# Reordered lead-in of a routed-attention and MLP-mixer kernel: q's first rows turned ahead of the centroids, one PSUM buffer each for the clusters of k and q

## The chip, the core and the metric

One core of a Trainium2 chip runs the whole kernel. The metric is device time in microseconds (us) of one execution; the kernel before takes 845.08 us, the median of four executions (844.96 to 846.0).

## What is computed

The reference is routed attention followed by an MLP mixer, all in float32. There are 4 batches, 8 heads, 768 positions, 64 elements per head and 16 centroids per head:

```
q_assign = argmax_c (q/|q|) . (centroid_c/|centroid_c|)      # the same for k
scores   = 0.125 * q k^T where q_assign == k_assign, else -1e9
attn     = softmax(scores) @ v                               # heads side by side: x, 768 x 512
u        = x + (relu(x^T @ w_tok1) @ w_tok2)^T
out      = u + relu(u @ w_ch1) @ w_ch2
```

The setup draws all inputs at random; no centroid is zero.

## The kernel before

The work has two parts. The first treats 16 pairs of heads (4 batches by 4 pairs), one after another; the second is the mixer. TensorE works through both almost without a pause. All instructions stand in each engine's queue in the order in which the program issues them, so an instruction that waits holds up everything behind it on its engine.

For a pair of heads the kernel needs q and k turned, with the head's elements on the partitions (the tile `qkT`), and the cluster of each position of q and k as a one-hot row, turned as well (`ohT`). The scores of the pair (line 422) are two products that add up in PSUM: the one-hot rows of k by those of q, where q's are multiplied by a large negative number, and then k by q. k's one-hot rows are inverted, so the first product is zero for positions of the same cluster. ScalarE takes the exponential of each such tile (line 429), VectorE adds them up (line 437), and TensorE multiplies them by v (line 447). One pass of scores has two halves of q (`qh`) by six blocks of k (`j`).

From the second pair on, turning is done by VectorE (line 292, on rows loaded in quarters by line 141) and by DMA (line 347), during the pair before. The first pair has no pair before it, and the function `begin` prepares it in another way, which I call the lead-in:

- The centroids (`cen`, line 795) and the rows of q and k of the first pair (`load_first`, line 365) are loaded. k's four loads stand in SyncE's queue behind the centroids, q's four in ScalarE's queue. Each has one head's share of one half `n` of the rows. Behind k's loads SyncE issues the loads of the second pair (line 141) and of v (line 150).
- Meanwhile TensorE multiplies a tile of zeros by itself (`keep_warm`, line 813), 12 times at first and a few times between later steps.
- `centroids_norm` (lines 244 to 278) works out on VectorE, in 12 short instructions one behind the other, each centroid divided by its norm (lines 247 to 273; the third of these, line 250, keeps the squared norm above 2 to the power of -100). TensorE turns the result (line 277, tile `pc`). `centroids_out` (line 283) copies it in two parts to the tile `cnd`, from which the products with q and k are made, and line 821 copies it whole to `cnT`, which only a fallback reads.
- `turn_first(0)` (line 376) turns the first half of the rows on TensorE, three blocks of k and three of q. VectorE copies k (line 824) and ScalarE q (line 823) out of PSUM to `qkT`.
- `route_products` (line 302) multiplies the centroids by k and q of this half, and `route` (lines 318, 320, 323) finds each row's largest product and writes the one-hot rows, first k's and then q's.
- `turn_first(1)` turns the second half of the rows, and ScalarE copies both (line 830).
- `route_turn_first(0)` (line 386) turns the one-hot rows on TensorE, three blocks of k and three of q in one PSUM tile `po`. Then `route_first_out` has VectorE copy k's (line 396) and q's (line 394, with the multiplication).
- `route_products` and `route` follow for the second half of the rows, and the scores begin. Between the second and the third block of scores, `second_first` turns the one-hot rows of the second half.

Two PSUM pools matter. `ps_av` has two buffers, which its tiles take in turn: the target of `keep_warm`, `pc`, the two `po`, and then products of the next pair and `av`. `ps_sc` has three, for the turned rows, the products `pr` and the scores.

Of the kernel before, what the change touches and what calls it, by code (L numbers as in the profile page):

```python
# [8 lines left out]
F32 = mybir.dt.float32  # L9
BF16 = mybir.dt.bfloat16  # L10
U32 = mybir.dt.uint32
U16 = mybir.dt.uint16
I32 = mybir.dt.int32
# [6 lines left out]
P = 128  # L20
# [7 lines left out]
HJ = NJ // 2  # L28
HS = HJ * P
# [11 lines left out]
BIG = float(2**33)  # L41
# [7 lines left out]
def kernel(  # L49
# [29 lines left out]
    nc = tc.nc  # L79
# [5 lines left out]
    def pool(name, bufs, stack=None, **kw):  # L85
        return (stack or fast).enter_context(
            tc.tile_pool(name=name, bufs=bufs, reuse_waits="tile", **kw)
        )

    ps_av = pool("ps_av", 2, space=PSUM)  # L90
    ps_sc_stack = fast.enter_context(ExitStack())
    ps_sc = pool("ps_sc", 3, ps_sc_stack, space=PSUM)
# [16 lines left out]
    rsmall = pool("rsmall", 1, routing, side="right")  # L109
# [3 lines left out]
    ident = const.tile([P, P], F32, name="ident")  # L113
    identb = const.tile([P, P], BF16, name="identb")
# [3 lines left out]
    ohs = [rsmall.tile([P, 2, NJ, P], BF16, name=f"oh{i}", bufs=1) for i in range(2)]  # L118
# [9 lines left out]
    state = {}  # L128
# [17 lines left out]
    def load_v(g):  # L146
        b, f = divmod(g, NF)
        st = state[g]
        st["va"] = loads.tile([P, 2, NJ, D], F32, name="va")
        nc.sync.dma_start(  # L150
            st["va"], v[b, 2 * f : 2 * f + 2].rearrange("h (p j) d -> p h j d", p=P)
        )
# [91 lines left out]
    def centroids_norm(cen):  # L244
        sq = rsmall.tile([P, D], F32, name="censq")
        ss = rsmall.tile([P, 1], F32, name="ss")
        nc.vector.tensor_tensor(out=sq, in0=cen, in1=cen, op=ALU.mult)
        nc.vector.reduce_sum(out=ss, in_=sq, axis=AX.X)
        lo = rsmall.tile([P, 1], F32, name="lo")
        nc.vector.tensor_scalar_max(out=lo, in0=ss, scalar1=float(2.0**-100))  # L250


        nrm = rsmall.tile([P, 1], F32, name="nrm0")
        nc.vector.tensor_scalar(
            out=nrm.bitcast(I32), in0=lo.bitcast(I32), scalar1=0.5, scalar2=float(0x1FBB6875),
            op0=ALU.mult, op1=ALU.add,
        )
        for it in range(2):
            rr = rsmall.tile([P, 1], F32, name="rr")
            nc.vector.reciprocal(out=rr, in_=nrm)  # L260
            tw = rsmall.tile([P, 1], F32, name="tw")
            nc.vector.scalar_tensor_tensor(
                out=tw, in0=ss, scalar=rr, in1=nrm, op0=ALU.mult, op1=ALU.add
            )
            nrm = rsmall.tile([P, 1], F32, name="nrm")
            nc.vector.tensor_scalar(
                out=nrm, in0=tw, scalar1=(0.5, 0.49984956)[1 - it], scalar2=(0.0, 1e-6)[it],
                op0=ALU.mult, op1=ALU.add,
            )
        rden = rsmall.tile([P, 1], F32, name="rden")  # L270
        nc.vector.reciprocal(out=rden, in_=nrm)
        cn = rsmall.tile([P, 2, D], F32, name="cn")
        nc.vector.tensor_scalar_mul(
            out=cn, in0=cen.unsqueeze(1).to_broadcast([P, 2, D]), scalar1=rden
        )
        pc = ps_av.tile([P, H * C], F32, tag="av", name="pc")
        nc.tensor.transpose(out=pc, in_=cn.rearrange("p i d -> p (i d)"), identity=ident)
        return pc

    def centroids_out(pc):  # L280
        for i in range(2):
            rows = slice(i * D, (i + 1) * D)
            nc.vector.tensor_copy(
                out=cnd[rows, :, i], in_=pc.rearrange("p (f i c) -> p f i c", f=NF, i=2)[rows, :, i]
            )
# [44 lines left out]
    def route_count(g, js=slice(0, NJ), column=None):  # L330


        column = g if column is None else column
        nc.scalar.activation(
            out=rsmall.tile([P, NJ, 2, C], BF16, name="others")[:, js], in_=onehots(g, 1, js),
            func=ACT.Copy, accum_out=cells[:, column : column + 1],
        )
# [16 lines left out]
    def load_first():  # L354
        st = state[0] = {}
        st["T"] = qktp.tile([P, 2, NJ, P], F32, name="qkT")
        st["ohT"] = qktp.tile([P, 2, NJ, P], BF16, name="ohT")
        st["rows"] = [
            work.tile([P, 2, HS], F32, name="ex").rearrange("p a (j h d) -> p a j h d", h=2, d=D)
            for _ in range(2)  # L360
        ]
        for n in range(2):
            for a, src, queue in ((1, k, nc.sync), (0, q, nc.scalar)):
                for h in range(2):
                    queue.dma_start(
                        st["rows"][n][:, a, :, h],
                        src[0, h].rearrange("(p j) d -> p j d", p=P)[:, HJ * n : HJ * n + HJ],
                    )

    def turn_first(n, tiles):  # L370

        st = state[0]
        js = slice(HJ * n, HJ * n + HJ)
        for a in (1, 0):
            for j in range(HJ):
                nc.tensor.transpose(
                    out=tiles[a][:, j * P : (j + 1) * P],
                    in_=st["rows"][n][:, a, j].rearrange("p h d -> p (h d)"), identity=ident,
                )
        return [(st["T"][:, a, js].rearrange("p j t -> p (j t)"), tiles[a]) for a in range(2)]  # L380

    def route_turn_first(n):
        po = ps_av.tile([P, 2, HJ, P], BF16, tag="av", name="po")
        for a in (1, 0):
            for j in range(HJ):
                nc.tensor.transpose(
                    out=po[:, a, j], in_=ohs[0][:, a, HJ * n + j], identity=identb
                )
        return po

    def route_first_out(n, po, a):
        out = state[0]["ohT"][:, a, HJ * n : HJ * n + HJ]
        if a == 0:
            nc.vector.tensor_scalar_mul(out=out, in0=po[:, 0], scalar1=-BIG)  # L394
        else:
            nc.vector.tensor_copy(out=out, in_=po[:, 1])

    def second_first():

        po = route_turn_first(1)  # L400
        for a in (1, 0):
            route_first_out(1, po, a)
        for n in range(2):
            route_count(0, slice(HJ * n, HJ * n + HJ), NPAIR * n)
        nc.vector.tensor_tensor(
            out=cells[:, 0:1], in0=cells[:, 0:1], in1=cells[:, NPAIR : NPAIR + 1], op=ALU.add
        )
        state[0].pop("rows")
# [384 lines left out]
    def begin():  # L793
        cen = rsmall.tile([P, D], F32, name="cen")
        nc.sync.dma_start(cen, centroids.rearrange("h c d -> (h c) d"))
        load_first()

        nc.vector.memset(ones, 1.0)
        warm = rsmall.tile([P, WMAX], BF16, name="warm")
        nc.vector.memset(warm, 0.0)  # L800
        nc.vector.memset(cnd, 0.0)
        nc.scalar.activation(out=rsmall.tile([P, QP], F32, name="expd"), in_=ones, func=ACT.Exp)
        make_identity(nc, ident)
        nc.gpsimd.tensor_copy(out=identb, in_=ident)
        for oh in ohs:
            nc.gpsimd.memset(oh, 0.0)
        load(1)
        load_v(0)
        pw = ps_av.tile([P, HS], F32, tag="av", name="av")

        def keep_warm(n):
            for _ in range(n):
                nc.tensor.matmul(pw, lhsT=warm[:, 0:P], rhs=warm[:, P : P + HS], start=True, stop=True)

        js = [slice(0, HJ), slice(HJ, NJ)]
        keep_warm(12)
        pc = centroids_norm(cen)
        keep_warm(2)
        scs = [ps_sc.tile([P, 2, 512], F32, tag="sc", name="pt") for _ in range(2)]
        centroids_out(pc)  # L820
        nc.scalar.copy(out=cnT, in_=pc)
        tq, tk = turn_first(0, [x[:, 0, 0:HS] for x in scs])
        nc.scalar.copy(out=tq[0], in_=tq[1])
        nc.vector.tensor_copy(out=tk[0], in_=tk[1])
        keep_warm(2)
        pr = ps_sc.tile([P, 2, 512], F32, tag="sc", name="pr")
        route_products(0, pr[:, 0, 0 : HS // 2], js[0])
        pt = ps_sc.tile([P, 2, 512], F32, tag="sc", name="pt")
        for out, src in turn_first(1, [pt[:, a, 0:HS] for a in range(2)]):
            nc.scalar.copy(out=out, in_=src)  # L830
        route(0, js[0])
        keep_warm(3)
        po = route_turn_first(0)
        for a in (1, 0):
            route_first_out(0, po, a)
        route_products(0, pr[:, 1, 0 : HS // 2], js[1])
        route(0, js[1])

# [325 lines left out]
```

## Time and profile before

| | before |
|---|---|
| median of four executions | 845.08 us (844.96 to 846.0) |
| the profiled execution | 845.76 us |
| its span, first to last instruction | 844.0 us |
| mean granted clock of TensorE | 1.000 |
| TensorE busy | 834.3 us (99%) |
| VectorE busy | 501.8 us (59%) |
| ScalarE busy | 374.8 us (44%) |
| first matmul of scores of the first pair | starts at 11.14 us |

The profile is that of one execution. All places in time are microseconds from the first instruction. PE is TensorE's matmuls and PEld its weight loads, DVE is VectorE, ACT ScalarE, POOL GpSimd, and SP SyncE; a "q" behind an engine's name is its sequencer, which issues DMAs. `qkT<-pt` reads: writes tile qkT from tile pt. L422 is line 422. A row of the timeline gives the start, the time to the end of its last instruction, the engine, the line, the operation, the tiles, the shapes, the number of instructions and, in brackets, how long the engine was idle before it and for whom. A row of the chain of waits gives start, length and what the end of the program was waiting for at that time.

### The profile page before, as it was taken

What the parts mean: (1) busy time and instruction counts of PE and PEld (TensorE: products, weight loads), DVE (VectorE), ACT (ScalarE), POOL (GpSimd) and SP (SyncE); (2) the same over time, 40 slices, a digit from 0 to 9 for tenths busy, and PEclk for the clock granted to TensorE, in tenths of its full rate; (3) what the DMA queues carried; (4) which work ended last, traced back from release to release, by engine and by line L of the source; (5) the groups of instructions that cost most, each with busy time, mean ns of one, the idle gap of its engine ahead of it and who ended that gap; (6) DMA issues with size and microseconds to landing.
All of it is one profiled execution on the core that took longest, in us unless ns stands there. A gap on an engine that the chain in (4) does not pass through costs nothing.

```text
span 844.0 us, 10784 instructions
## 1 busy us (share of the span) xinstructions
PE 834.3 (99%) x4102; PEld 507.1 (60%) x4102; DVE 501.8 (59%) x848; ACT 374.8 (44%) x570; POOL 45.6 (5%) x40
## 2 busy tenths in 40 slices
PE   9999999999999999999999999999999999999997
PEld 4444444444444444444577686785876867768676
DVE  6879898989898862893653434423454333443342
ACT  5678777777777762453210352104612035220210
POOL 1001010101101000430000000000000000000000
PEclk9999999999999999999999999999999999999999
DMA  8786666868675412541000040000310012200001
GB/s 152 148 149 143 125 138 123 169 130 159 146 138 125 57 44 69 162 110 29 0 1 1 19 105 27 0 1 19 82 51 0 1 19 47 85 1 0 1 15 64
DMA packets 183963, 60.19 MB, mean 71 GB/s; under 512 B 172768, under 2 KB 176864, under 8 KB 183904
## 3 DMA queue, kind: packets, MB, share of 16 engines
q1 hardware_dynamic: 182304, 59.04, 33.0%
q8 instruction: 34, 0.56, 0.3%
q10 hardware_dynamic: 1600, 0.39, 0.2%
q14 instruction: 25, 0.20, 0.1%
HBM read 34.64 MB, written 6.29 MB: 48 GB/s over the span
## 4 chain that ended last, share of the span: by engine, by line
PE 92%; DVE 5%; DMA 1%; ACT 0%; issue 0%; SPq 0%; DVEq 0%
PE sc L422 18%; PE pX L740 15%; PE pX L689 15%; PE av L447 13%; PE pZ L689 7%; PE pZ L740 7%; PE ph L527 4%; PE pY L740 4%; PE pY L689 4%; PE pu L536 3%; PE small L483 1%; DVE wh L215 1%; PE small L302 1%; DVE wT L220 1%; DVE wh L210 1%; DVE x L539 1%
## 5 line engine op out<-in xcount | busy, mean ns | idle before, releaser
L429 ACT ACTIVATE ex<-sc 128x768 f32<-128x768 f32 x192 | 149.2, 811 | 27.7 <-PE sc L422 16.1
L422 PE MATMUL sc<-qkT 64*128 64x384 f32 x768 | 155.1, 482 | 0.0
L437 DVE TENSOR_TENSOR sum<-sum,ex 128x768 f32<-128x768 f32 x128 | 127.7, 998 | 27.4 <-ACT ex L429 15.2
L447 PE MATMUL av<-ex,va 128*64 128x384 f32 x768 | 127.4, 488 | 0.0
L447 PEld LDWEIGHTS av<-ex,va 128*64 128x64 f32 x768 | 53.8, 137 | 71.7 <-issue 69.0
L422 PEld LDWEIGHTS sc<-qkT 64*128 64x128 f32 x768 | 68.5, 187 | 36.3 <-issue 35.6
L697 ACT COPY p<-pX 128x384 f32<-128x384 f32 x24 | 11.4, 475 | 138.7 <-PE pX L689 120.5
L689 PE MATMUL pX<-uT,wc 128*128 128x384 f32 x192 | 67.4, 487 | 0.0
L422 PE MATMUL sc<-ohT 64*128 64x384 bf16 x384 | 63.3, 324 | 0.5 <-DVE ohT L394 0.2
L689 PEld LDWEIGHTS pX<-uT,wc 128*128 128x128 f32 x192 | 36.2, 190 | 24.7 <-issue 1.0
L454 ACT COPY avrows<-av 128x768 uint16<-128x768 uint16 x32 | 25.5, 796 | 47.1 <-PE av L447 47.1
L227 POOL TENSOR_TENSOR wc<-wT,wup 128x512 int32<-128x512 int32 x24 | 33.0, 1376 | 191.4 <-DVE wT L220 189.7
L527 PE MATMUL ph<-x,wt 128*128 128x512 f32 x96 | 41.9, 594 | 0.8 <-DVE x L539 0.8
L610 ACT COPY uT<-ucols 128x768 uint16<-128x768 uint16 x32 | 33.5, 1051 | 20.7 <-DMA ucols<-urows 20.7
L422 PEld LDWEIGHTS <-ohT 64*128 64x128 bf16 x384 | 20.1, 94 | 35.9 <-issue 11.1
L536 PE MATMUL pu<-h,wt 128*128 128x512 f32 x96 | 41.7, 592 | 0.0
L553 DVE TENSOR_TENSOR c<-pZ,u 128x384 f32<-128x384 f32 x24 | 13.4, 558 | 46.8 <-PE pZ L689 46.8
L708 ACT ACTIVATE hA<-hA 128x384 f32<-128x384 f32 x24 | 12.6, 523 | 63.4 <-DVE hA L553 63.4
L553 DVE TENSOR_TENSOR x<-pX,x 128x256 f32<-128x256 f32 x24 | 10.2, 423 | 42.8 <-PE pX L740 42.8
L689 PE MATMUL pZ<-uTs,w1s 128*128 128x384 f32 x96 | 35.0, 487 | 0.4 <-DVE uTs L550 0.4
L740 PE MATMUL pX<-wc,hA 128*128 128x256 f32 x144 | 35.0, 379 | 0.0
L740 PE MATMUL pZ<-w2s,hS 128*128 128x256 f32 x144 | 35.0, 379 | 0.0
(121 smaller groups left out, 1224.9 us busy)
## 6 DMA issues: line engine op xcount, KB each, us to landing
raw<-in_moe_w_ch_dram SPq DMA_DIRECT2D x24, 512.0 KB, 4.2
va<-in_v_dram SPq DMA_DIRECT2D x16, 384.0 KB, 3.6
out_dram<-x SPq DMA_DIRECT2D x24, 256.0 KB, 2.1
qk<-in_k_dram SPq DMA_DIRECT2D x60, 96.0 KB, 3.8
qk<-in_q_dram SPq DMA_DIRECT2D x60, 96.0 KB, 3.5
raw<-in_moe_w_tok_dram SPq DMA_DIRECT2D x3, 512.0 KB, 4.6
raw<-in_moe_w_tok_dram SPq DMA_DIRECT2D x4, 384.0 KB, 3.8
ucols<-urows SPq DMA_TRANSPOSE x32, 2.8
```

The source lines that it names most:

```text
L227: nc.gpsimd.tensor_tensor(out=dst.bitcast(I32), in0=T, in1=up, op=ALU.add)
L422: nc.tensor.matmul(sc[:, h, 0:HS], lhsT=src[rows, 1, j], rhs=src[rows, 0, js], start=start, stop=not start,)
L429: nc.scalar.activation(out=ex, in_=sc[:, :, 0:HS], func=ACT.Exp, scale=SM_SCALE)
L437: nc.vector.tensor_tensor(out=acc, in0=acc if j > 1 else st["ex", qh, 0], in1=st["ex", qh, j], op=ALU.add)
L447: nc.tensor.matmul(av[h * D : (h + 1) * D], lhsT=st["va"][:, h, j], rhs=ex[:, h], start=(j == 0), stop=(j == NJ - 1),)
L454: nc.scalar.copy(out=st["rows"][:, qh], in_=av.bitcast(U16).rearrange("p (t w) -> p w t", w=2))
L527: nc.tensor.matmul(pf, lhsT=W["tok1"][:, j, t * P : (t + 1) * P], rhs=xs[b][:, j], start=(j == 0), stop=(j == NJ - 1),)
L536: nc.tensor.matmul(pu, lhsT=W["tok2"][:, t, j], rhs=h1s[b][:, t], start=(t == 0), stop=(t == NT - 1))
L553: nc.vector.tensor_tensor(out=dst, in0=a, in1=b, op=ALU.add)
L610: nc.scalar.copy(out=out, in_=pools.pop(("ucols", i)).rearrange("p w j t -> p w (j t)"))
L689: nc.tensor.matmul(psum, lhsT=A[a][:, k, c * P : (c + 1) * P], rhs=R[r][:, k], start=start and k == 0, stop=k == 1, skip_group_check=not s ...
L740: nc.tensor.matmul(psum, lhsT=h2[a][:, k, i * P : (i + 1) * P], rhs=Bw[w][:, 3 * part + k], start=start and k == 0, stop=k == 2, skip_grou ...
```

## The change

Four things are done in the lead-in, and nothing outside of it:

1. One of the first 12 idle multiplications is taken out, and the two between the centroids and the turning. q's first rows are turned ahead of the centroids' products and copied by ScalarE at once; k's are turned behind the centroids. The copy to `cnT` moves behind k's turning.
2. The instruction that keeps the squared norm above a small number is taken out.
3. The second half of the rows is turned with q first and k second. As before, ScalarE's copies stand behind all six.
4. The one-hot rows of k and of q get a PSUM buffer each. The copy of each is issued right behind its three turns; for the first half, ScalarE copies k's (VectorE did it before).

```diff
-        lo = rsmall.tile([P, 1], F32, name="lo")
-        nc.vector.tensor_scalar_max(out=lo, in0=ss, scalar1=float(2.0**-100))
...
-            out=nrm.bitcast(I32), in0=lo.bitcast(I32), scalar1=0.5, scalar2=float(0x1FBB6875),
+            out=nrm.bitcast(I32), in0=ss.bitcast(I32), scalar1=0.5, scalar2=float(0x1FBB6875),
...
-    def turn_first(n, tiles):
+    def turn_first(n, a, out):
 
         st = state[0]
+        for j in range(HJ):
+            nc.tensor.transpose(
+                out=out[:, j * P : (j + 1) * P],
+                in_=st["rows"][n][:, a, j].rearrange("p h d -> p (h d)"), identity=ident,
+            )
         js = slice(HJ * n, HJ * n + HJ)
+        return st["T"][:, a, js].rearrange("p j t -> p (j t)"), out
+
+    def route_turn_first(n):
+
         for a in (1, 0):
+            po = ps_av.tile([P, HJ, P], BF16, tag="av", name="po")
             for j in range(HJ):
...
+                nc.tensor.transpose(out=po[:, j], in_=ohs[0][:, a, HJ * n + j], identity=identb)
+            out = state[0]["ohT"][:, a, HJ * n : HJ * n + HJ]
+            if a == 0:
+                nc.vector.tensor_scalar_mul(out=out, in0=po, scalar1=-BIG)
+            elif n == 0:
+                nc.scalar.copy(out=out, in_=po)
+            else:
+                nc.vector.tensor_copy(out=out, in_=po)
...
-        keep_warm(12)
+        keep_warm(11)
+        scs = [ps_sc.tile([P, 2, 512], F32, tag="sc", name="pt") for _ in range(2)]
+        tq = turn_first(0, 0, scs[0][:, 0, 0:HS])
+        nc.scalar.copy(out=tq[0], in_=tq[1])
         pc = centroids_norm(cen)
-        keep_warm(2)
-        scs = [ps_sc.tile([P, 2, 512], F32, tag="sc", name="pt") for _ in range(2)]
         centroids_out(pc)
+        tk = turn_first(0, 1, scs[1][:, 0, 0:HS])
+        nc.vector.tensor_copy(out=tk[0], in_=tk[1])
         nc.scalar.copy(out=cnT, in_=pc)
-        tq, tk = turn_first(0, [x[:, 0, 0:HS] for x in scs])
-        nc.scalar.copy(out=tq[0], in_=tq[1])
-        nc.vector.tensor_copy(out=tk[0], in_=tk[1])
         keep_warm(2)
         pr = ps_sc.tile([P, 2, 512], F32, tag="sc", name="pr")
         route_products(0, pr[:, 0, 0 : HS // 2], js[0])
         pt = ps_sc.tile([P, 2, 512], F32, tag="sc", name="pt")
-        for out, src in turn_first(1, [pt[:, a, 0:HS] for a in range(2)]):
+        for out, src in [turn_first(1, a, pt[:, a, 0:HS]) for a in (0, 1)]:
             nc.scalar.copy(out=out, in_=src)
         route(0, js[0])
         keep_warm(3)
-        po = route_turn_first(0)
-        for a in (1, 0):
-            route_first_out(0, po, a)
+        route_turn_first(0)
```

More of the change, by code (lines that the diff above doesn't have):

```diff
@@ L368, in load_first @@
                     )
-    def turn_first(n, tiles):
+    def turn_first(n, a, out):
         st = state[0]
+        for j in range(HJ):
[3 more added lines that the diff above has]
+            )
         js = slice(HJ * n, HJ * n + HJ)
+        return st["T"][:, a, js].rearrange("p j t -> p (j t)"), out
+    def route_turn_first(n):
         for a in (1, 0):
+            po = ps_av.tile([P, HJ, P], BF16, tag="av", name="po")
             for j in range(HJ):
[L376 to L383, printed above, removed]
-        for a in (1, 0):
[L385 to L396, printed above, removed]
+                nc.tensor.transpose(out=po[:, j], in_=ohs[0][:, a, HJ * n + j], identity=identb)
[6 more added lines that the diff above has]
+                nc.vector.tensor_copy(out=out, in_=po)
     def second_first():
-        po = route_turn_first(1)
-        for a in (1, 0):
-            route_first_out(1, po, a)
+        route_turn_first(1)
         for n in range(2):
@@ L832, in begin @@
         keep_warm(3)
-        po = route_turn_first(0)
-        for a in (1, 0):
-            route_first_out(0, po, a)
+        route_turn_first(0)
         route_products(0, pr[:, 1, 0 : HS // 2], js[1])
```

## The prediction, written before the changed kernel ran

> **What bounds the kernel now.** I read the page first: busy time by engine, and the shares of the chain of waits.
>
> ```profile
> PE 834.3 (99%) x4102; PEld 507.1 (60%) x4102; DVE 501.8 (59%) x848; ACT 374.8 (44%) x570; POOL 45.6 (5%) x40
> ...
> PE 92%; DVE 5%; DMA 1%; ACT 0%; issue 0%; SPq 0%; DVEq 0%
> ```
>
> TensorE is the bound. A change to the lead-in can only pay by letting the first pair's scores (L422) start earlier; from there TensorE runs to the end. So I looked for what could hold time in place behind the lead-in. TensorE's own waits, in a list for the whole span, are few: 0.8 us at L527, 0.5 at L302, 0.4 at L689, 0.2 at L422, and those of the lead-in. The 0.5 us at L302 (31.48 us) waits for VectorE, whose work goes back through additions and routing to a product that TensorE makes at 21.48 us. It moves along when TensorE does. The others wait for VectorE too, in chains that start with TensorE's results.
>
> Then I read the chain of waits from the start to 13 us:
>
> ```profile
> 2.72 0.24 DVE censq L247
> ...
> 3.24 0.17 DVE lo L250
> ...
> 5.09 0.30 DVE cn L273
> 5.39 0.14 issue
> 5.53 0.45 PE pc L277
> 5.97 0.64 PE av L813 x2
> 6.61 0.95 PE pt L376 x6
> 7.56 0.02 issue
> 7.58 0.49 ACT qkT L823
> 8.07 0.04 issue
> 8.11 0.53 PE pr L302 x8
> ...
> 10.46 0.04 DVE ohT L396
> 10.49 0.24 issue
> 10.73 0.36 DVE ohT L394
> 11.09 0.04 issue
> 11.14 1.79 PE sc L422 x12
> ```
>
> The reader is to see one chain through four engines. The centroids land at 2.70, VectorE normalises them until 5.38, TensorE turns them, does two multiplications of zeros (L813), turns six blocks, ScalarE copies q, and at 8.11 the products begin. Their routing ends in two VectorE copies, one behind the other (L396, L394), and at 11.14 the scores begin. The timeline of the two copies of turned rows shows who is late:
>
> ```profile
> 7.26 0.56 DVE L824 COPY qkT<-pt 128x384 f32<-128x384 f32 x1 [0.79 <-PE pt L376]
> 7.58 0.48 ACT L823 COPY qkT<-pt 128x384 f32<-128x384 f32 x1 [0.75 <-PE pt L376]
> ```
>
> k is copied by 7.82 and q by 8.06: q comes last, though its rows have long been there (ScalarE issues its first two loads at 0.74 and 1.24, with 2.3 and 2.9 us to landing: 3.0 and 4.1).
>
> **The change, step by step** (times in the profiled execution).
>
> *One multiplication less, q turned first.* The twelfth opening multiplication starts at 4.73; in its place the first block of q is turned. Its rows are there since 4.1, 0.6 us of cover. The first two turns of L376 started 0.21 us apart and took 0.42 each (6.41, 6.61). Three end at 4.73 + 0.42 + 0.42 = 5.57. ScalarE's last work before that ends at 4.38, so it copies from 5.61 to 6.09. q then is far from the end of the chain.
>
> *The clamp.* L250 starts at 3.24, the next instruction at 3.43: 0.19 us go, all on the path. `cn` ends at 5.19 instead of 5.38. TensorE started `pc` 0.15 us after that, so at 5.34; three turns before it occupy TensorE until 4.73 + 3 x 0.21 = 5.36. So `pc` runs from 5.36 to 5.81, and the two copies to `cnd` (started 0.04 later, 0.46 together) end at 6.31. Queued behind `pc` on TensorE are k's turns; they cost nothing more here.
>
> *k behind the centroids.* After `pc` the next TensorE instruction started 0.24 us later (5.53 to 5.77), so k's turns start at 5.60 and end at 6.44. k's second load was issued by 1.67 and took 3.0: there at 4.7. VectorE copies from 6.48 (free since 6.31) to 7.04, and the products follow 0.05 later, at 7.09 instead of 8.11. That is **1.02 us** off. The two multiplications behind k's turns (0.32 apart in the opening group) are issued by 6.9 and delay nothing. The copy to `cnT` is on ScalarE, idle then.
>
> *Routing and the order of the second half.* From the products to the second one-hot result (L323 ends at 10.02) nothing changes: 9.00. The second half's last load lands at 3.2 + 3.7 = 6.9 at the latest, and is used from about 7.9. ScalarE's two copies (L830, 9.49 to 10.35) move to 8.47 to 9.33, a little earlier if q's needn't wait for k's turns.
>
> *Separate buffers.* The row that sets this price is the copies' wait:
>
> ```profile
> 10.46 0.36 DVE L396 COPY ohT<-po 128x384 bf16<-128x384 bf16 x1 [0.44 <-PE po L386]
> 10.73 0.35 DVE L394 TENSOR_SCALAR ohT<-po 128x384 bf16<-128x384 bf16 x1
> ```
>
> Before, VectorE needs from 10.46 to 11.08 for both, and it starts only after all six turns (9.91 to 10.42). Now q's turns end at 9.40, VectorE multiplies from 9.44 to 9.79, and the scores start 0.06 later (as 11.08 to 11.14): 9.85. Beside it ScalarE copies k's: three of the six turns (0.51 us together, 0.22 each, so 0.06 apart) end 0.34 after the first, at 9.23; ScalarE is free at 9.33 at the latest. It has no such bf16 copy in this trace. The nearest rows are its float32 copy of the same 128x384 (0.48) and VectorE's bf16 one (0.36); I take 0.48. It ends at 9.75 to 9.81, and the scores could start at 9.86 at worst. The products of the second half need 0.53 of TensorE from about 9.26 and end at 9.79, under the same cover. So this part takes off **0.27 us** more, and the scores start at 9.85 instead of 11.14: **1.29 us** in all.
>
> *What the separate buffers add* is a wait: `ps_av` has two buffers, so the turns of the second half's k (TensorE, with the scores' third block queued behind them) must wait for ScalarE's copy. They started 1.72 us after the first scores (12.86 after 11.14), so at 11.57; the copy is done at 9.8. The cover is 1.8 us. Their one-hot rows must be ready too: products end at 9.79, VectorE took 1.23 us (11.00 to 12.24), so 11.07, with 0.5 us to spare. In the second half VectorE still copies both, and TensorE did not wait there before.
>
> *Behind the lead-in.* No DMA is moved and no queue of SyncE or POOL is passed. What stays fixed in time is the loads. VectorE turns the second pair's rows at 14.66, then at 13.4; the last of these loads was issued at about 8.6 and took 3.7: 12.3. v of the first pair was issued at 9.32 and took 4.0: 13.3, used at 22.26, then at 21.0. SyncE issues loads until 18.52 and then waits for VectorE until 24.63. All covers hold, and the 1.29 us should arrive at the end whole.
>
> **The clock in the lead-in.** The rows of L813 show TensorE slower at first: 527 ns for each of its matmuls up to 6.1 us, 326 ns from 7.4 us. L376 goes from 421 to 272 ns about 7 us into the span. My sum assumes that this stays at about 7.0. If it came early, before 5.4, the kernel before would gain more than the changed one: by the faster rows (turns 0.11 apart, 0.27 each; L813 0.16 apart) its products would start at about 7.36 (0.75 earlier) and the changed kernel's at about 6.76 (0.33 earlier, VectorE's chain holding it). The gain would be 1.29 - 0.75 + 0.33 = 0.87. If it came at 8.1, products, q's turns and idle multiplications run slower in both, and the gain is about 1.4.
>
> [...]
>
> **The number.** Against the profiled execution: 845.76 - 1.29 = 844.47. Against the median, 0.68 lower, the same step gives 843.79, and the smallest of the clock cases, 0.87, gives 844.2. I predict **844.2 us**, a change of 0.1%. Here 0.2%, about what a measurement of this kernel can tell from no change, is 1.69 us.
>
> **Rivals.**
>
> *The clock comes later* (slower side). With full speed only after 10 us, the products are 0.3 late, the six turns of the second half end at about 9.0 (0.21 apart), the three idle multiplications at 10.0 (0.32 apart), and only then come the one-hot turns. Scores start at about 11.3, 0.1 later than before, so 845.2 to 846.0. From there each us without full speed costs 0.5 us, as scores run at half the rate. It decides for "slower by over 0.2%" only if full speed comes after about 14 us. For it: fewer zero multiplications ahead, turns in their place. Against it: turns were there before the switch already, and TensorE now has no gap at 5.25 to 5.53. Chance 0.15, of which 0.03 beyond 846.8.
>
> *The gain is covered elsewhere*: a load or VectorE holds the second pair back, and the 31.48 us wait grows by what the start won: 845.1. For it: VectorE is busy 3.7 of 4 us there. Against it: its chain starts from TensorE. Chance 0.06.
>
> *The separate buffers don't do what they say*: if ScalarE's copy waits for all six turns, it runs from 9.44 to 9.92 and scores start at 9.97: 0.12 less gain, 844.3. Inside the forecast.
>
> *More than counted*: the medians fall on a late clock before and an early one after; 11.14 + 0.35 before against 9.5 after would be 2.0 us, 843.1. Chance 0.10.
>
> The forecast, 843.7 to 844.7, has 0.69. Range: 843.4 to 845.3. Faster by over 0.2%: 0.10; within: 0.87; slower: 0.03.
>
> **What would show it.** q's copy ends near 6.1 and k's near 7.0; the products start near 7.1; ScalarE copies the one-hot rows beside VectorE's multiplication; the first L422 starts near 9.85 and the L302 wait of 0.5 us comes near 30.2. I am wrong if L422 starts after 10.5, if L813's rows of 527 ns reach beyond 8 us, or if a new TensorE wait stands between 10 and 32 us.

## The result, and the profile after

The changed kernel takes **844.26 us** (median of 40 executions, 843.90 to 844.95), the kernel before 845.18 us (60 executions, 844.75 to 846.0). The ratio is 0.9989, with a 95% interval of 0.9985 to 0.9993: 0.92 us less, inside the 0.2% that counts here as no change, and clear of zero. The profiled execution of the changed kernel took 844.12 us with a span of 842.3 us. (Three single executions lay far outside, 1794 us of the kernel before and 3955 and 5052 us of e4 below; they are left out of all ratios.)

The chain of waits in the lead-in of the changed kernel; its lines have moved by a few (L422 is L416 now, L302 is L301, L824 is L817):

```profile
2.73 0.24 DVE censq L247
...
4.92 0.30 DVE cn L272
...
5.26 0.34 PE pc L276
...
5.62 0.22 DVE cnd L282
...
5.85 0.23 DVE cnd L282
...
6.11 0.57 DVE qkT L817
6.68 0.14 issue
6.82 0.53 PE pr L301 x8
...
9.11 0.52 PE pr L301 x8
9.63 1.72 PE sc L416 x12
```

ScalarE's copy of q and TensorE's six turns in a row have left the chain. VectorE's work on the centroids, with one turn by TensorE (`pc`) in its midst, now goes through to k's copy, and the products start at 6.82 us instead of 8.11. The scores start at 9.57 instead of 11.14, by the timeline. The 1.57 us arrive later: TensorE's wait at 31.48 us is at 29.89 (1.59), the one at 371.44 at 369.82 (1.62), and the span is 1.6 us shorter. The first wait in TensorE's timelines, before and after:

```profile
31.48 0.85 PE L302 MATMUL small<-qkT,cnd 128*32 128x384 f32 x8 [0.47 <-DVE qkT L292]
```

```profile
29.89 0.85 PE L301 MATMUL small<-qkT,cnd 128*32 128x384 f32 x8 [0.46 <-DVE qkT L291]
```

But the medians differ by 0.92 only. The two profiled executions are not alike, and the rows of the idle multiplications in the changed kernel, ahead of q's turns and behind k's, show why:

```profile
L807 PE MATMUL av<-warm x6: 527/528/528, 2.5 to 4.1; 128*128 128x384 bf16 x6
```

```profile
L807 PE MATMUL av<-warm x2: 326/326/326, 5.8 to 6.0; 128*128 128x384 bf16 x2
```

The three numbers are the shortest, median and longest duration in ns. At 5.8 us TensorE is at full speed here; in the kernel before it was slow still at 6.1 (527 ns). The record of the granted clock gives the moments: 7.05 us in the profile before, 4.53 in this one. So the profiles set a late clock against an early one, and a part of the 1.57 us belongs to the clock, not to the change. With a late clock on both sides 1.19 us are left (11.14 against 9.95 in e7 below, whose lead-in is the changed one); with an early one on both sides about 0.8 (10.18 in e3 and the 0.19 of the clamp, against 9.57). The 0.92 of the medians lies between.

### The profile page after: what moved, and what is told of

Its sections match the earlier page's. It is cut to its first block, busy times and chain, and to the rows that moved or that the text cites. A ratio compares the mean times of both kernels' runs of the same rounds, so it can differ in the third digit from the quotient of the medians.

```text
span 842.3 us, 10776 instructions
## 1 busy us (share of the span) xinstructions
PE 832.8 (99%) x4099; PEld 506.4 (60%) x4099; DVE 501.4 (60%) x846; ACT 375.0 (45%) x571; POOL 45.6 (5%) x40
## 4 chain that ended last, share of the span: by engine, by line
PE 86%; DVE 10%; DMA 1%; SPq 1%; issue 1%; ACT 0%; POOL 0%; DVEq 0%; POOLq 0%
PE pX L734 15%; PE pX L683 15%; PE sc L416 15%; PE av L441 11%; PE pZ L683 7%; PE pZ L734 7%; PE ph L521 4%; PE pY L734 4%; PE pY L683 4%; PE pu L530 3%; DVE sum L431 2%; DVE wT L220 1%; DVE wh L215 1%; PE small L477 1%; DVE wh L210 1%; PE small L301 1%
## 5 line engine op out<-in xcount | busy, mean ns | idle before, releaser
L416 PE MATMUL sc<-qkT 64*128 64x384 f32 x768 | 155.1, 482 | 0.0
L416 PEld LDWEIGHTS sc<-qkT 64*128 64x128 f32 x768 | 68.5, 187 | 36.1 <-issue 35.3
L416 PE MATMUL sc<-ohT 64*128 64x384 bf16 x384 | 63.3, 324 | 0.3 <-DVE sim L317 0.2
L521 PE MATMUL ph<-x,wt 128*128 128x512 f32 x96 | 41.9, 594 | 0.8 <-DVE x L533 0.8
L416 PEld LDWEIGHTS <-ohT 64*128 64x128 bf16 x384 | 20.3, 94 | 35.7 <-issue 11.1
L734 PE MATMUL pX<-w2s,hA 128*128 128x256 f32 x144 | 35.0, 379 | 0.0
```

The lines of the kernel that those rows point to most:

```text
L416: nc.tensor.matmul(sc[:, h, 0:HS], lhsT=src[rows, 1, j], rhs=src[rows, 0, js], start=start, stop=not start,)
L521: nc.tensor.matmul(pf, lhsT=W["tok1"][:, j, t * P : (t + 1) * P], rhs=xs[b][:, j], start=(j == 0), stop=(j == NJ - 1),)
L734: nc.tensor.matmul(psum, lhsT=h2[a][:, k, i * P : (i + 1) * P], rhs=Bw[w][:, 3 * part + k], start=start and k == 0, stop=k == 2, skip_grou ...
```

## The experiments

The theory to test was that of the prediction: the parts bring what they take off the start of the scores, and all that follows moves along rigidly. Against it stood that one part brings it all, that the clock does, and that something later takes a part back. Ratios are to the kernel before in the same session, whose medians were 845.14, 845.05 and 845.16 us.

| kernel | median us | ratio, 95% interval | full speed at | products at | scores at |
|---|---|---|---|---|---|
| before | 845.18 | 1 | 7.05 | 8.11 | 11.14 |
| changed | 844.26 | 0.9989 (0.9985 to 0.9993) | 4.53 | 6.82 | 9.57 |
| e1_order | 844.75 | 0.9993 (0.9984 to 1.0002) | 7.07 | 7.17 | 10.19 |
| e2_split | 845.03 | 0.9995 (0.9986 to 1.0004) | 6.84 | 8.00 | 10.75 |
| e3_clamp | 845.00 | 0.9995 (0.9986 to 1.0004) | 5.28 | 7.16 | 10.18 |
| e4_k_early | 843.46 | 0.9978 (0.9969 to 0.9988) | 4.79 | 6.19 | 8.94 |
| e5_no_idle | 845.70 | 1.0009 (1.0000 to 1.0019) | 11.74 | 7.03 | 11.12 |
| e6_k_scalar | 843.66 | 0.9982 (0.9973 to 0.9992) | 4.45 | 6.37 | 9.12 |
| e7_one_less | 844.12 | 0.9988 (0.9979 to 0.9997) | 6.93 | 7.20 | 9.95 |
| e8_one_more | 844.50 | 0.9992 (0.9983 to 1.0001) | 4.74 | 6.89 | 9.64 |
| e9_k_early_2 | 843.68 | 0.9982 (0.9972 to 0.9991) | 6.50 | 6.76 | 9.51 |
| e10_k_early_11 | 844.05 | 0.9985 (0.9976 to 0.9994) | 7.14 | 7.07 | 9.83 |

The last three columns are those of the one profiled execution.

### The parts by themselves

**e1_order**: the changed kernel with one PSUM tile for both one-hot rows, as before:

```diff
-            po = ps_av.tile([P, HJ, P], BF16, tag="av", name="po")
+        po = ps_av.tile([P, 2, HJ, P], BF16, tag="av", name="po")
...
-            elif n == 0:
-                nc.scalar.copy(out=out, in_=po)
```

> The changed kernel with its part 4 undone: the one-hot rows of k and q share one PSUM buffer again and VectorE copies both, one behind the other. Theory (each part is worth what it takes off the start of the scores, and everything later moves along): the scores start 0.27 us later than in the changed kernel for the same moment of the clock, so the time is 844.26 + 0.27 = 844.5. Rival (the separate buffers do nothing, ScalarE's copy waits for all six turns anyway): 844.3 to 844.4. Rival (the gain comes from the clock, which the order brings forward): 844.3, with full speed near 4.5 us again.

**e2_split** has that part alone, on the kernel before (the same edit the other way round).

> The kernel before with part 4 alone: a PSUM buffer each for the one-hot rows of k and q, k's copied by ScalarE for the first half. Theory: the scores start 0.27 us earlier than before for the same moment of the clock, so 845.18 - 0.27 = 844.9. Rival (ScalarE is late, since its two copies of the second half stand ahead): 845.0 to 845.2. Rival (the order alone brought the gain): 845.2.

**e3_clamp** is the kernel before without L250:

```diff
-        nc.vector.tensor_scalar_max(out=lo, in0=ss, scalar1=float(2.0**-100))
...
-            out=nrm.bitcast(I32), in0=lo.bitcast(I32), scalar1=0.5, scalar2=float(0x1FBB6875),
+            out=nrm.bitcast(I32), in0=ss.bitcast(I32), scalar1=0.5, scalar2=float(0x1FBB6875),
```

> The kernel before without the instruction that keeps the squared norm above a small number (part 2 alone). Theory: VectorE's chain from the centroids sets the end, so its 0.19 us arrive at the end: 845.18 - 0.19 = 845.0. Rival (TensorE's turns and idle multiplications hold the copies anyway, as the moment of the clock does): 845.2.

Measured: 844.75, 845.03 and 845.00 us. The signs fit, e1 is 0.25 later than expected, and 11 executions each can't tell 0.1 us apart. The traces can. From the products to the scores it takes 3.02 us before, in e1 and in e3, and 2.75 or 2.76 in the changed kernel and in e2: the separate buffers bring the 0.27 us to the row. From the start of L247 to that of `cn` it takes 2.37 us before and 2.18 in the changed kernel and in e3: the clamp's 0.19. e1, with full speed at 7.07 us, stands beside the kernel before at 7.05: order and clamp together bring its products from 8.11 to 7.17. The order alone was not run; 0.75 is the difference. And the clock: e3 is the kernel before, without the clamp, at 5.28 us of clock, and its products start 0.95 earlier than those of the profile before, 0.19 of it the clamp, so 0.76 for 1.8 us of clock (the prediction had 0.75).

But the same traces show a thing that no theory had. TensorE's wait at L302, 0.47 us before and 0.46 in the changed kernel, is 0.89 in e1 and e2 and 0.88 in e3. The list of TensorE's waits and VectorE's timeline of e3 (its L300 is L302, its L435 is L437):

```profile
PE small L300 <- DVE qkT L290: 0.9, 1, 0.9
```

```profile
24.56 3.08 DVE L435 TENSOR_TENSOR sum<-sum,ex 128x768 f32<-128x768 f32 x3
28.17 0.96 DVE L435 TENSOR_TENSOR sum<-sum,ex 128x768 f32<-128x768 f32 x1 [0.53 <-DVE sum L435]
```

VectorE, in the midst of five equal additions, stands still for 0.53 us, and the wait is named for VectorE itself. In the changed kernel the same additions run through (4.14 us for four). So e1 to e3 start early and give back 0.41 us at 31 us. Near 167 us they get 0.33 of it back: the kernels before and after wait there, and they don't. Where does a pause come from that goes away with one instruction?

### Pauses of VectorE, 128 records apart

Counting VectorE's records in the traces, its sequencer's waits included, the pauses stand behind the 63rd record in e1, e2 and e3, and behind the 191st and 319th in the kernels before and after: 128 apart. Each addition is two records, a wait of the sequencer (a record of its own, 0.02 us long) for the addition before it, and the addition. In these traces the pause costs VectorE time where such a wait is the last of its 128: the next record starts 0.40 to 0.48 us after the wait ends, with nothing left to run (158.37 to 158.77 in the kernel before). Where the addition is the last, the pause passes while the addition runs: in the changed kernel the 63rd record, an addition, starts at 27.13 and ends at 28.09, and the 64th, a wait for something else, starts at 27.60. One instruction more or less turns the one into the other: VectorE has 1207 records before, 1205 in the changed kernel, 1206 in e1 to e3. The third place costs TensorE time too. VectorE's and TensorE's timelines of the changed kernel:

```profile
156.85 0.96 DVE L431 TENSOR_TENSOR sum<-sum,ex 128x768 f32<-128x768 f32 x1
158.27 3.09 DVE L431 TENSOR_TENSOR sum<-sum,ex 128x768 f32<-128x768 f32 x3 [0.46 <-DVE sum L431]
```

```profile
166.61 0.34 PE L416 MATMUL sc<-ohT 64*128 64x384 bf16 x2 [0.17 <-DVE sim L317]
```

Products of the one-hot rows start about 0.81 us apart in this stretch, and this one starts 1.14 us behind the one before it (165.47): 0.33 us lost. The kernel before has the same two waits (0.46 at 158.77, 0.16 at 168.17). Its first one is named for ScalarE's `ex`, but VectorE's wait for that had ended at 158.37. Two experiments change the count in a place where VectorE is idle. **e7_one_less** fills the tile of ones on GpSimd, and the exponential that reads it moves behind that (it still runs at 4.15 us):

```diff
-        nc.vector.memset(ones, 1.0)
...
-        nc.scalar.activation(out=rsmall.tile([P, QP], F32, name="expd"), in_=ones, func=ACT.Exp)
...
+        nc.gpsimd.memset(ones, 1.0)
+        nc.scalar.activation(out=rsmall.tile([P, QP], F32, name="expd"), in_=ones, func=ACT.Exp)
```

> The changed kernel with one VectorE instruction fewer in an idle place: the tile of ones is filled by GpSimd instead, before anything waits for it. The lead-in's chain is the same. Theory (pause at every 128th place): the pause now falls between instructions that don't wait, TensorE's wait at 166.6 us goes, and 844.26 - 0.33 = 843.9. Rival (the pauses follow the time or the loads, not the count of instructions): 844.26, with the wait at 166.6 us still there.

**e8_one_more** adds one fill on VectorE, long before the centroids land:

```diff
+        nc.vector.memset(rsmall.tile([P, 1], F32, name="spare"), 0.0)
```

> The changed kernel with one VectorE instruction more in an idle place, a fill of 128x1 at about 1.3 us. Theory (pause at every 128th place): VectorE's additions pause by 0.47 us near 26 to 27 us, TensorE's wait near 30 us grows from 0.46 to 0.87, and the wait at 166.6 us goes: 844.26 + 0.41 - 0.33 = 844.34. Rival (the pauses have to do with something else): both waits as in the changed kernel, 844.26.

VectorE's and TensorE's timelines of e7:

```profile
157.23 4.15 DVE L431 TENSOR_TENSOR sum<-sum,ex 128x768 f32<-128x768 f32 x4
```

```profile
166.66 0.33 PE L416 MATMUL sc<-ohT 64*128 64x384 bf16 x2
```

and of e8:

```profile
24.02 3.08 DVE L431 TENSOR_TENSOR sum<-sum,ex 128x768 f32<-128x768 f32 x3
27.64 0.96 DVE L431 TENSOR_TENSOR sum<-sum,ex 128x768 f32<-128x768 f32 x1 [0.54 <-DVE sum L431]
```

```profile
30.41 0.85 PE L301 MATMUL small<-qkT,cnd 128*32 128x384 f32 x8 [0.89 <-DVE qkT L291]
```

In e7 the four additions run through and TensorE's wait is gone; in e8 the pause stands at 27 us and TensorE waits 0.89 us. Set against the changed kernel, scores of the pairs before 166 us start 0.38 later in e7's trace (its clock is late) and those behind 0.05: 0.33 us gone. In e8's the first pair's scores start 0.08 later than in the changed kernel and the second pair's 0.51, so 0.43 are lost between, and 0.33 go at 166 us. That is the theory's pattern in both, and the rival's in neither. In the medians it is smaller than the clock's scatter: 844.12 (expected 843.9) and 844.50 (844.34). Part of e7's shortfall is in its trace: the wait at L521, 370 us, is 0.89 us instead of 0.75. Why that one varies (0.75 to 0.89 over all profiles) I did not find out. For e1 to e3 the pauses cost 0.41 - 0.33 = 0.08 us in all, so they don't explain the 0.25 of e1.

In all twelve profiles, with a pause that costs or without, one 8 KB read on a queue that carries instructions follows 1.1 to 2.4 us after the 63rd, 191st and 319th record (28.93 us in e3, 27.96 in e6), and 8 KB by 128 would be 64 bytes a record, an estimate from these two figures. So the place looks like the border between two blocks of instructions; that is argued, not shown. The pause itself isn't this read: in e3 VectorE goes on at 28.17, before it. What happens in the pause stays open.

### The rival: a clock that comes later

**e5_no_idle** is the changed kernel without its three groups of idle multiplications:

```diff
-        keep_warm(11)
...
-        keep_warm(2)
...
-        keep_warm(3)
```

> The changed kernel without any multiplication of zeros in the lead-in; TensorE's first work is then the turning of q at about 4.1 us. It measures the rival of the prediction, a clock that comes later. If turns count as work for the clock, full speed comes 3.3 to 6.7 us after 4.1 (from the profiles so far: 3.3 to 5.8 after TensorE's first matmul), the lead-in runs slow, the scores start at about 10.1 instead of 9.57, and part of them runs at half rate: 844.7 to 845.3. If only the dense scores count, full speed comes after 13.5 us, and each us until then costs another 0.5 us: 846 or more.

It takes 845.70 us, between the two expected ranges, and inside the 845.2 to 846.0 of the prediction's rival. TensorE's timeline:

```profile
10.32 0.87 PE L301 MATMUL pr<-qkT,cnd 128*32 128x192 f32 x8 [0.31 <-ACT qkT L822]
11.12 0.50 PE L416 MATMUL sc<-ohT 64*128 64x384 bf16 x2
11.41 0.97 PE L416 MATMUL sc<-qkT 64*128 64x384 f32 x4
12.22 0.32 PE L416 MATMUL sc<-ohT 64*128 64x384 bf16 x2
```

The scores start at 11.12 (the prediction's rival said about 11.3 for full speed after 10 us), run slow (1.10 us from the first products of the one-hot rows to the next, against 0.81 from 13.57 to 14.38), and are at speed by 12.2. The clock came at 11.74, 7.6 us after TensorE's first work and 0.6 after the first scores. So it did not wait for more than these 0.6 us of dense scores; that the turns and products ahead of them counted is argued from this. The 6.7 us and the 13.5 us that were expected were the author's estimates, and no run shows them: the profiles until then had 3.3 to 5.8 us from the first matmul to full speed. The clock also came later after the first work than in any kernel with idle multiplications (3.2 to 5.9 us). The rival's price fits, 1.4 us over the changed kernel; its condition is not met in any of the eleven other profiles, which have idle multiplications: full speed comes between 4.4 and 7.2 us there.

### A version that is faster

With the early clock VectorE's chain now holds the products through k's copy. **e6_k_scalar** gives that copy to ScalarE:

```diff
-        nc.vector.tensor_copy(out=tk[0], in_=tk[1])
+        nc.scalar.copy(out=tk[0], in_=tk[1])
```

> The changed kernel with k's first copy on ScalarE, behind q's, at the same place in TensorE's queue. Theory 1 (lead-in): the copy no longer waits for the centroids' copies on VectorE; with an early clock the products start at about 6.52 instead of 6.82, so 0.2 to 0.3 us off. Theory 2 (every 128th place in VectorE's instruction stream has a pause of 0.4 to 0.5 us that costs only where a wait stands last ahead of it): VectorE has one instruction fewer ahead of the first pair's additions, so the pause at 158 us goes behind other work and another 0.33 us go. Both: 843.6 to 843.75. Theory 1 alone: 844.0. Theory 2 alone: 843.9.

843.66 us, as for both theories together, and 0.18% under the kernel before. ScalarE's and TensorE's timelines:

```profile
5.83 0.48 ACT L817 COPY qkT<-pt 128x384 f32<-128x384 f32 x1 [0.23 <-PE pt L373]
```

```profile
6.37 0.53 PE L301 MATMUL pr<-qkT,cnd 128*32 128x192 f32 x8 [0.24 <-ACT qkT L817]
```

The products start 0.45 us earlier than in the changed kernel (0.11 of it from centroids that landed earlier in this execution), and behind the ninth pair's start another 0.33 are gone with the pause.

**e4_k_early** turns k ahead of the centroids too, after ten opening multiplications:

```diff
-        keep_warm(11)
+        keep_warm(10)
...
+        tk = turn_first(0, 1, scs[1][:, 0, 0:HS])
+        nc.scalar.copy(out=tk[0], in_=tk[1])
         pc = centroids_norm(cen)
         centroids_out(pc)
-        tk = turn_first(0, 1, scs[1][:, 0, 0:HS])
-        nc.vector.tensor_copy(out=tk[0], in_=tk[1])
```

> The changed kernel, in which k's first rows too are turned ahead of the centroids and copied by ScalarE behind q's, with ten opening multiplications instead of eleven; VectorE then has the centroids alone. Theory (VectorE's chain from the centroids through the copy of k holds the products; the clock only shifts it): with an early clock the products start when the centroids' copies end, at about 6.15 instead of 6.82, and with a late one TensorE's slow turns delay the centroids, 6.7 instead of 7.1. So 0.4 to 0.65 us off: 843.6 to 843.9. Rival (ScalarE's two copies or k's landing at 4.7 take the place of VectorE): 844.2. Rival (the clock comes later with more turns among the opening work): 844.5 or more, with full speed after 8 us.

Two repeats asked what its two long executions were, and whether its tight start matters:

> The kernel with k's first rows turned ahead of the centroids and copied by ScalarE, once more and unchanged: two of its eleven executions had taken 3955 and 5052 us. If that was a disturbance from outside, all are near 843.4 to 843.5 now; if it belongs to the kernel (k's rows are turned within 0.2 us of their landing at 4.63 us), about two in eleven are over 3900 us again.

> The same with eleven opening multiplications, so that all turns start 0.32 us later while the clock is low. With an early clock the centroids' turn is hardly later (5.29 instead of 5.25) and the time is near 843.5; with a late one it waits for six slow turns until 6.0 and the products start 0.3 us later than with ten: 843.5 to 844.0. If the long executions come from turning k right when it lands, they are fewer or none here; if they come from the order of the work, about two in eleven.

e4 has 843.46 us (843.41 without the two), its repeat e9 843.68 with no long execution in eleven, and e10 844.05. e4's products start at 6.19, for 6.15 expected. The time is below the expected 843.6 to 843.9 because the theory left out the pause: against the changed kernel e4's scores start 0.63 earlier before 166 us and 0.96 behind. The long ones did not come again; the kernel before had one of 1794 us beside e9 and e10. I take them for disturbances, and their cause stays open. e10 shows what was expected of slow turns: the centroids' turn starts at 6.01 and the products at 7.07, in e9 with ten multiplications at 5.70 and 6.76. In both, full speed comes only behind the centroids' turn (7.14 and 6.50). e4 and e9 together are no faster than e6 by more than the scatter, and e6 asks less of the loads.

## Why the prediction was right

Point by point:

- *The sum of the lead-in.* 7.09 for the products and 9.85 for the scores were worked out for a clock at 7.05. The lead-in that met it is e7's, the changed one at 6.93: 7.20 and 9.95. Up to the end of k's copy the sum holds to 0.01 us (7.05 for 7.04). The 0.1 us too little is the step from there to the products: 0.05 was taken, as behind ScalarE's copy of q before, and behind VectorE's copy it took 0.15 here and 0.14 in the changed kernel's profile. VectorE's row and two of TensorE's in e7:

```profile
6.49 0.56 DVE L817 COPY qkT<-pt 128x384 f32<-128x384 f32 x1 [0.18 <-PE pt L373]
```

```profile
7.20 0.53 PE L301 MATMUL pr<-qkT,cnd 128*32 128x192 f32 x8
9.95 0.34 PE L416 MATMUL sc<-ohT 64*128 64x384 bf16 x2
```

  At the early clock 6.76 and 9.5 were said, and 6.82 and 9.57 came. q is copied by 5.64 there, far ahead, and k, as said, comes last.
- *The clamp and the separate buffers* brought 0.19 and 0.27 us. ScalarE's bf16 copy, the one unknown price, took 0.48 us like the float32 one, beside VectorE's 0.36 for the other row. ScalarE's timeline of the changed kernel:

```profile
8.98 0.48 ACT L390 COPY ohT<-po 128x384 bf16<-128x384 bf16 x1
```

- *q first in the second half* brought nothing, as allowed for: ScalarE's two copies start at 8.19, 0.04 after the sixth turn.
- *The clock* decided the size. The choice of 844.2 between 843.8 and 844.5 rested on the gain being 0.87 with an early clock and 1.29 with a late one; the medians give 0.92. That full speed could come at another moment than the 7.05 us of the one trace at hand was the author's estimate. No run shows it at 8.1 us, where a gain of about 1.4 was put, or at 10 us; the runs showed it between 4.45 and 7.14 us in the eleven profiles with idle multiplications and at 11.74 us without any. No trace showed that most executions are like the early case: the prediction took the smallest of its gains, and that 844.2 is off by no more than 0.06 us is in part luck. In 86 executions of the kernel before, timed beside the experiments, the 18 with a mean granted clock of 1.000 (as in its profiled execution) have a median of 845.76 us, and the other 68, between 844.84 and 845.54, one of 845.06. That is the 0.7 us by which the profiled execution stood over the median. That these 18 had a late clock is argued: in the profiles the mean counts only what is lost behind the stretch at full clock, at the end (1.000 before, though TensorE was slow until 7.05 us), and for one length of the stretch a late end is a late start.
- *"Behind the lead-in" was right only for this change.* The step said that all covers hold and what the start wins arrives whole. It does here, 1.57 at the scores and 1.62 at 371 us. But for the clamp or the buffers alone it would have been wrong by 0.41 us at 31 us, though 0.33 come back at 166 us. The two edits together take two instructions from VectorE, and with two the waits fall as before; that was luck. One wait of the prediction's list, 0.2 us at L422 (168.17 us), was said to come from TensorE's results; it hangs on the pause behind the 319th record, and went in e7. I had counted what the instructions cost and not that they are counted.
- *The rivals.* The late clock's price fits e5, but in the changed kernel it did not come. The rival of a gain covered at L302 has a mechanism, the pause, but not in this kernel.

## What to carry to other kernels

Read from the profile whether the execution that it shows is a typical one: here a clock that came late made 0.7 us of an execution that was taken as the base, and the gain in time was six tenths of the gain between two traces. A change of 0.1% needs its parts priced in the trace, at the place where the chain meets TensorE, since the medians of eleven executions don't tell 0.1 us from nothing. And an instruction removed from an engine moves all that follow it by one place: where a wait that the profile names for the engine itself appears or goes, count its instructions before looking for a cause in the data.

## What the runs showed of the hardware

- VectorE's sequencer stopped for 0.40 to 0.48 us at places 128 records apart (63, 191 and 319), and VectorE was idle by it only where a wait that held it up stood last ahead of the place. Its idle time was then 0.46 to 0.54 us, against 0.10 between other additions (seen in seven profiles; e7 and e8 moved it by one instruction).
- The stretch at full clock has a length of 836.265, 832.852 or 829.439 us in all twelve profiles: it differs by 3.413 us and by nothing between, and 836.265 is 245 times that. So both ends of the stretch sit on one grid of 3.413 us, as far as these lengths tell. Its place differs from one execution to the next: full speed came at 4.53 us in the changed kernel's profile and at 6.93 in e7's, with the same lead-in.
- Turns in place of multiplications of zeros, which the prediction named for a later clock, were not seen to delay it: in the eight profiles that have turns in place of some of the multiplications full speed came 3.2 to 5.9 us after TensorE's first matmul, in the three with the old order 4.0 to 5.8. In e5, with turns, small products and 0.6 us of scores, it came after 7.6 us.
